# A WKV recurrence with a two-layer network behind it: pairs' exponents in PSUM, wider masks, and a written-out order of all steps

## The chip, the cores and the metric

One core of a Trainium2 chip runs the whole program. The time is device microseconds of one execution; three runs of the kernel before were taken. An execution of it was also profiled, and times inside it count from its first instruction.

## The reference

Inputs are r, k, v, w of shape (batch 4, heads 8, steps 768, 48), a bonus vector u (8, 48), and two weight matrices of 384 x 2048 and 2048 x 384. All are float32.

```python
for t in range(S):
    cur = einsum('bhd,bhe->bhde', u * k[t], v[t])
    y[t] = einsum('bhd,bhde->bhe', r[t], state + cur)
    state = w[t][..., None] * state + einsum('bhd,bhe->bhde', k[t], v[t])
x = y.transpose(0, 2, 1, 3).reshape(3072, 384)
h = x @ w_in
out = maximum(0.01 * h, h) @ w_out
```

## The kernel before

**Two stages.** The 768 steps of each batch are cut into chunks of 128, which makes 24 chunks in all. The first stage turns a chunk into 128 rows of x, transposed, in the tile `xT`. The second stage is the network: `up` (L1128) multiplies `xT` by `w_in` for a block of one or two chunks, `g` (L1143) applies the leaky function on ACT, `down` (L1155) multiplies by `w_out`, a copy (L1166 on DVE, L1168 on ACT) brings the result from PSUM to the tile `o`, and a store (L1172) sends it.

**A single chunk** (`single`, chunks 4 to 23). Four loads (L903, one each for w, k, r, v, 192 KB) fill a tile of the pool `in`, of which there are seven. ACT takes the logarithm of w (L913), PE forms cumulative sums (L919, with the totals in L922), DVE adds to make `ci` (L931), ACT takes exponentials (L945, L949; L940 for the totals), DVE multiplies r and k by them (L579, tile `rk`), and PE transposes the products (L590, with copies L595 and L597) or a transposing DMA does (L971, L1067). PE multiplies them into scores (L1076), DVE masks the scores (L995, 512 columns), PE multiplies the masked scores and the state by v (L1036, L1031). POOL computes the bonus (L611, L615, L623; the sum L619 on DVE), casts v (L631) and scales the state (L982). DVE adds the bonus (L654), and the rows are transposed into `xT` by PE (L640, copies L645, L647) or by DMA (L1052, L1089).

**A pair** (`pair`, chunks 0 and 1, then 2 and 3) does two chunks of one batch at once, the steps interleaved in two lots j = 0, 1. Its loads are L669, its logarithm L688, its cumulative sums L697 into three banks `c1`, `c0`, `cg`, its totals L714. Four exponentials (L733) follow: into a fourth bank `e0`, in place in `c1` and `cg`, and, from `c0`, into the SBUF tile `er0` of the pool `ci`. Four products (L579) read these. Then come transposes, scores (L823), masks (L834), the products with v (L781, L843), and copies (L881, L883). Pair 0 does this in two halves of two head groups (`PARTS`); both halves use the same four banks. For every half and each lot there is a scores step and two mask steps, of 256 columns in pair 0:

```python
for x, (g0, g1) in enumerate(parts):
    for js in range(2):
        ...
        for par in range(2):
            ... m.t[:, par, g0:g1, :], in0=sc[par]..., in1=mask2[:, js, :]...
```

**Weights** come in ten loads (L509 and L514 for the two matrices) through the same seven `in` tiles and are cast to bfloat16 on DVE, ACT or POOL (L533, L535, L531). An `in` tile is free again when its last reader is done.

**u** is loaded by ACT's queue, split in three (L559), spread over the partitions by three matmuls (L566), and copied (L575).

**Order.** All instructions are issued in an order fixed when the program is built. The class `Plan` runs a list scheduler over 1074 steps with written-in durations, priorities (`RANK`), some engines forced (`FORCE`), limits on banks, and a model of the DMA queue; each engine then runs its steps in that order, and SP issues loads, stores and transposing DMAs in one queue. Where the plan leaves PE idle in the first 24 us, matmuls on a tile `zeros` (L1197) are put in, into a PSUM bank held for them until the third chunk's `up`.

Of the kernel before, what the change touches and what calls it, by code (L numbers as in the profile page):

```python
# [12 lines left out]
AX = mybir.AxisListType  # L13


class Buf:


    def __init__(self, pool, kind=None, wide=1):
        self.pool, self.kind, self.users, self.t, self.free_at = pool, kind or pool, [], None, 0.0  # L20
        self.wide, self.written, self.other = wide, 0.0, 0.0


class Whole:


    def __init__(self, buf):
        self.buf = buf

    @property  # L30
    def t(self):
        return self.buf.t.rearrange("p x g t -> p (x g t)").rearrange("p (g c) -> p g c", c=256)


class Half:


    def __init__(self, buf, x):
        self.buf, self.x = buf, x

    @property
    def t(self):
        return self.buf.t[:, self.x]


class Plan:


    ENGINES = ("PE", "DVE", "ACT", "POOL", "SP")
    OVER = {"PE": 0.0, "DVE": 0.08, "ACT": 0.11, "POOL": 0.04, "SP": 0.0}  # L50
    BEGIN = {"PE": 1.1, "DVE": 2.9, "ACT": 0.8, "POOL": 4.9, "SP": 0.8}
    SEEN = {"PE": 0.21, "DVE": 0.05, "ACT": 0.05, "POOL": 0.07, "SP": 0.05}

    def __init__(self, limits, slack_from, slack, late):
        self.steps, self.limits, self.late = [], limits, late
        self.slack_from, self.slack = slack_from, slack

    def add(self, engs, fn, pri, deps=(), reads=(), takes=(), wire=None):
        i = len(self.steps)
        self.steps.append([engs, fn, pri, {d for d in deps if d is not None}, tuple(reads), tuple(takes), wire])  # L60
        for b in (*reads, *takes):
            b.users.append(i)
        return i

    def order(self, pools):
        n = len(self.steps)
        users = [[] for _ in range(n)]
        left = [len(s[3]) for s in self.steps]
        for i, s in enumerate(self.steps):
            for j in s[3]:  # L70
                users[j].append(i)
        bufs = {}
        for i, s in enumerate(self.steps):
            for b in (*s[4], *s[5]):
                bufs[id(b)] = b
        remain = {k: len(b.users) for k, b in bufs.items()}
        for b in bufs.values():
            b.written = b.other = 0.0
        free_tiles = {p: [(0.0, k) for k in range(len(t))] for p, t in pools.items()}
        in_use = {}  # L80
        ready_at = [0.0] * n
        self.start, self.done, self.eng = [None] * n, [0.0] * n, [None] * n
        free = dict(self.BEGIN)
        ready = {e: [] for e in self.ENGINES}
        events = []
        dma_free, flying = 0.0, []

        def offer(i, t):
            for e in self.steps[i][0]:
                heapq.heappush(events, (t, 0, e, i))  # L90

        for i in range(n):
            if not left[i]:
                offer(i, 0.0)
        for e in self.ENGINES:
            heapq.heappush(events, (free[e], 1, e, -1))
        count, out = 0, []
        while events:
            now, kind, e, i = heapq.heappop(events)
            same = {e}  # L100
            if kind == 0 and self.start[i] is None:
                heapq.heappush(ready[e], (self.steps[i][2], i))
            elif kind == 2:
                in_use[i] -= 1
            while events and events[0][0] <= now + 1e-9:
                _, kind, e, i = heapq.heappop(events)
                same.add(e)
                if kind == 0 and self.start[i] is None:
                    heapq.heappush(ready[e], (self.steps[i][2], i))
                elif kind == 2:  # L110
                    in_use[i] -= 1
            for e in self.ENGINES:
                if (e not in same and "*" not in same) or free[e] > now + 1e-9:
                    continue
                held, chosen = [], None
                while ready[e]:
                    pri, i = heapq.heappop(ready[e])
                    if self.start[i] is not None:
                        continue
                    ok, given, left_free = True, [], {}  # L120
                    for b in (*self.steps[i][4], *self.steps[i][5]):
                        if b.pool == "ps" and b.t is not None:
                            until = b.other if e == "PE" else b.written
                            if until > now + 1e-9:
                                heapq.heappush(events, (until, 1, e, -1))
                                ok = False
                    for b in self.steps[i][5] if ok else ():
                        if b.t is None:
                            if in_use.get(b.kind, 0) >= self.limits.get(b.kind, 99):
                                ok = False  # L130
                                break
                            if b.pool not in left_free:
                                left_free[b.pool] = {k: f for f, k in free_tiles[b.pool] if f <= now + 1e-9}
                            have = left_free[b.pool]
                            at = [(max(have[k + x] for x in range(b.wide)), k) for k in have
                                  if all(k + x in have for x in range(b.wide))]
                            if not at:
                                ok = False
                                break
                            k = min(at)[1]  # L140
                            given.append((b, k))
                            for x in range(b.wide):
                                del have[k + x]
                    if ok:
                        chosen = i
                        break
                    held.append((pri, i))
                for h in held:
                    heapq.heappush(ready[e], h)
                if chosen is None:  # L150
                    continue
                i = chosen
                engs, fn, pri, deps, reads, takes, wire = self.steps[i]
                for b, k in given:
                    gone = range(k, k + b.wide)
                    free_tiles[b.pool] = [x for x in free_tiles[b.pool] if x[1] not in gone]
                    b.slot = k
                    b.t = pools[b.pool if b.wide == 1 else b.pool + " wide"][k]
                    in_use[b.kind] = in_use.get(b.kind, 0) + 1
                d = engs[e]  # L160
                self.start[i], self.eng[i] = now, e
                out.append(i)
                count += 1
                free[e] = now + d - (self.OVER[e] if d > 0.3 else 0.0)
                if wire is None:
                    self.done[i] = now + d + self.SEEN[e]
                    if self.slack_from <= pri < 1000:
                        self.done[i] += self.slack
                else:
                    wire, size, lat, lead = wire  # L170
                    while flying and sum(x for _, x in flying) + size > 150:
                        free[e] = max(free[e], flying.pop(0)[0])
                    dma_free = max(dma_free, free[e] + lead) + wire
                    flying.append((dma_free, size))
                    self.done[i] = dma_free + lat + (self.late if now > 20 else 0.0)
                for b in (*reads, *takes):
                    if e == "PE":
                        b.written = max(b.written, self.done[i])
                    else:
                        b.other = max(b.other, self.done[i])  # L180
                heapq.heappush(events, (free[e], 1, e, -1))
                for j in users[i]:
                    left[j] -= 1
                    ready_at[j] = max(ready_at[j], self.done[i])
                    if not left[j]:
                        offer(j, ready_at[j])
                for b in {id(b): b for b in (*reads, *takes)}.values():
# [164 lines left out]
def kernel(  # L352
# [11 lines left out]
    nc = tc.nc  # L364
# [867 lines left out]
```

## Time and profile before

| | |
|---|---|
| runs | 184.61, 185.21, 202.28 us; median 185.21 |
| span of the profiled execution | 183.7 us, 5052 instructions |
| its own time | not listed apart; the two lower runs lie 0.9 and 1.5 us above its span |
| busy | PE 175.3, PEld 129.6, DVE 118.1, ACT 115.3, POOL 98.8 us |
| DMA | 34.61 MB, mean 188 GB/s; 109682 of 117131 packets under 512 B |
| HBM | read 25.17 MB, written 4.72 MB |

The span is the time between the first and the last profiled instruction; a run's time has a little around it. PE's matmuls overlap, and their ends are modelled, so a matmul's listed duration is longer than the distance to the next one. The rows name a line of the kernel, an engine, and the tiles written and read. A row with SPq is an instruction that issues a transfer; its time is how long the issue took, not the transfer.

### The profile page before, as it was taken

Reading aid. Unit: us, or ns where it says so; the run is one execution under the profiler, and the core shown is the slowest. Engines: PE = TensorE matmul, PEld = TensorE weight load, DVE = VectorE, ACT = ScalarE, POOL = GpSimd, SP = SyncE. Lnnn points to the kernel's source line nnn. Section 1 sums busy time; section 2 is a strip of 40 time slices with the busy share of each in tenths; the row PEclk is TensorE's granted clock in tenths of the full one; section 3 lists DMA queues with packets and bytes.
Section 4 is the critical chain, followed back from the end, with each engine's and each line's share of the span. In section 5 each row is a group of like instructions: output and inputs, shape, how many; then the busy total and the mean of one; then the engine's idle time right before and its main releaser. Section 6 shows DMA issues by size and latency. Waiting matters only on the chain.

```text
span 183.7 us, 5052 instructions
## 1 busy us (share of the span) xinstructions
PE 175.3 (95%) x1974; PEld 129.6 (71%) x1974; DVE 118.1 (64%) x243; ACT 115.3 (63%) x259; POOL 98.8 (54%) x134
## 2 busy tenths in 40 slices
PE   7989999999999999999999999999999999899992
PEld 2545688856778786777877877777698866686860
DVE  7498983348976989999669395867675465261000
ACT  4844989868675597687772755874589920451722
POOL 6969411225869589986676284981149547000000
PEclk9999999999999999999999999999999999999999
DMA  5999679989999999999999999999499999803202
GB/s 128 273 275 333 199 222 382 325 159 195 179 171 177 173 160 189 192 186 177 215 191 161 204 177 203 152 222 190 126 243 234 190 245 253 216 2 46 86 0 87
DMA packets 117131, 34.61 MB, mean 188 GB/s; under 512 B 109682, under 2 KB 116339, under 8 KB 117107
## 3 DMA queue, kind: packets, MB, share of 16 engines
q1 hardware_dynamic: 117104, 34.28, 90.6%
q8 instruction: 15, 0.25, 0.6%
q14 instruction: 10, 0.07, 0.1%
q10 hardware_dynamic: 2, 0.00, 0.0%
HBM read 25.17 MB, written 4.72 MB: 163 GB/s over the span
## 4 chain that ended last, share of the span: by engine, by line
PE 56%; DMA 15%; SPq 9%; ACT 6%; DVE 6%; issue 4%; POOL 2%; DVEq 0%; POOLq 0%; ACTq 0%
PE ps L1128 23%; PE ps L1155 19%; SPq L903 9%; DMA in<-in_w_dram 5%; DMA in<-in_r_dram 4%; DMA in<-in_v_dram 4%; PE ps L1197 3%; DVE rk L579 2%; DMA xT<-y 2%; ACT g L1143 2%; PE ps L1076 2%; PE ps L1036 1%; PE ps L1031 1%; PE ps L919 1%; PE ps L823 1%
## 5 line engine op out<-in xcount | busy, mean ns | idle before, releaser
L1155 PE MATMUL ps<-w_out_b,g 128*128 128x384 bf16 x384 | 70.8, 326 | 0.1
L1128 PE MATMUL ps<-xT,w_in_b 128*128 128x256 bf16 (+1 forms) x672 | 69.4, 258 | 0.7 <-DMA xT<-y 0.7
L1143 ACT ACTIVATE g<-ps 128x512 bf16<-128x512 f32 x96 | 54.5, 605 | 20.3 <-PE ps L1128 16.4
L1128 PEld LDWEIGHTS <-w_in_b 128*128 128x128 bf16 x672 | 57.1, 98 | 9.0 <-DMA xT<-y 1.1
L1155 PEld LDWEIGHTS <-g 128*128 128x128 bf16 x384 | 34.8, 97 | 19.9 <-ACT g L1143 0.5
L579 DVE TENSOR_TENSOR rk<-in,ps 128x384 bf16<-128x384 f32 (+1 forms) x49 | 25.1, 525 | 11.3 <-DMA in<-in_r_dram 4.1
L995 DVE TENSOR_TENSOR m<-ps,maskb 128x512 bf16<-128x512 f32 x40 | 25.1, 683 | 9.1 <-PE ps L1076 9.1
L611 POOL TENSOR_TENSOR ru<-in,ub 128x384 f32<-128x384 f32 x24 | 23.9, 999 | 6.7 <-DMA in<-in_k_dram 6.5
L615 POOL TENSOR_TENSOR ru<-ru,in 128x384 f32<-128x384 f32 x24 | 24.3, 1016 | 3.1 <-DMA in<-in_r_dram 2.6
L623 POOL TENSOR_TENSOR vs<-in,dg 128x384 f32<-128x384 f32 x20 | 16.5, 828 | 10.9 <-DMA in<-in_v_dram 4.8
L982 POOL TENSOR_TENSOR sb<-s,a 128x384 bf16<-128x384 f32 x18 | 14.9, 829 | 13.3 <-ACT a L940 13.1
L1168 ACT COPY o<-ps 128x384 f32<-128x384 f32 x13 | 6.2, 478 | 15.5 <-PE ps L1155 15.4
L631 POOL CAST vb<-in 128x384 bf16<-128x384 f32 x24 | 12.1, 509 | 7.1 <-DMA in<-in_v_dram 7.1
L931 DVE TENSOR_TENSOR ci<-ps,lw 128x384 f32<-128x384 f32 x20 | 11.0, 554 | 7.0 <-PE ps L922 5.4
L619 DVE TENSOR_REDUCE dg<-ru 128x8 f32<-128x384 f32 x24 | 13.0, 547 | 3.6 <-POOL ru L615 3.5
L654 DVE TENSOR_TENSOR y<-ps,vs 128x384 bf16<-128x384 f32 x20 | 10.8, 553 | 3.1 <-PE ps L1036 1.7
L913 ACT ACTIVATE lw<-in 128x384 bf16<-128x384 f32 x20 | 10.2, 521 | 3.8 <-DMA in<-in_w_dram 3.7
L940 ACT ACTIVATE a<-ps 64x4 f32<-64x4 f32 x36 | 6.1, 168 | 9.1 <-DVE ci L931 6.0
L590 PE MATMUL ps<-ident,rk 128*128 128x128 bf16 x88 | 9.4, 235 | 1.8 <-DVE rk L579 1.7
L949 ACT ACTIVATE ps<-ci 128x384 f32<-128x384 f32 x20 | 9.8, 488 | 0.5 <-DVE ci L931 0.5
L945 ACT ACTIVATE ps<-ps 128x384 f32<-128x384 f32 x20 | 9.4, 472 | 0.5
L1166 DVE COPY o<-ps 128x384 f32<-128x384 f32 x11 | 6.1, 554 | 5.1 <-PE ps L1155 5.0
(89 smaller groups left out, 177.5 us busy)
## 6 DMA issues: line engine op xcount, KB each, us to landing
out_dram<-o SPq DMA_DIRECT2D x24, 192.0 KB, 3.5
in<-in_w_dram SPq DMA_DIRECT2D x22, 192.0 KB, 4.5
in<-in_k_dram SPq DMA_DIRECT2D x22, 192.0 KB, 4.4
in<-in_r_dram SPq DMA_DIRECT2D x22, 192.0 KB, 4.2
in<-in_v_dram SPq DMA_DIRECT2D x20, 192.0 KB, 4.1
in<-in_moe_w_out_dram SPq DMA_DIRECT2D x4, 768.0 KB, 9.3
in<-in_moe_w_in_dram SPq DMA_DIRECT2D x2, 768.0 KB, 6.8
in<-in_moe_w_in_dram SPq DMA_DIRECT2D x4, 384.0 KB, 7.8
```

The source lines that it names most:

```text
L579: (nc.gpsimd if e == "POOL" else nc.vector).tensor_tensor(out=o, in0=x, in1=i, op=ALU.mult)
L611: lambda e: nc.gpsimd.tensor_tensor(out=ru.t[:], in0=kv(), in1=ubv, op=ALU.mult),
L615: lambda e: nc.gpsimd.tensor_tensor(out=ru.t[:], in0=ru.t[:], in1=rv(), op=ALU.mult),
L619: lambda e: nc.vector.tensor_reduce(out=dg.t[:], in_=ru.t[:], axis=AX.X, op=ALU.add),
L623: lambda e: nc.gpsimd.tensor_tensor(out=vs.t[:], in0=vv(), in1=dg.t[:].unsqueeze(2).to_broadcast([128, H, D]), op=ALU.mult),
L631: {"POOL": 0.56}, lambda e: nc.gpsimd.tensor_copy(out=vb.t[:], in_=vv()),
L903: nc.sync.dma_start(out=part(i)(), in_=src[b, :, t0 : t0 + L, :].rearrange("h p d -> p h d"))
L982: lambda e: nc.gpsimd.tensor_tensor(out=sb.t[:].rearrange("p g a d -> p (g a) d"), in0=s_in.t[:].rearrange("p g a d -> p (g a) d"), in1=a_ ...
L995: lambda e, par=par: nc.vector.tensor_tensor(out=m.t[:, par, :, :], in0=sc[par].t[:].rearrange("p (g t) -> p g t", g=NP), in1=maskb[:].uns ...
L1128: nc.tensor.matmul(hp.t[:, a * N : (a + 1) * N].rearrange("p (s n) -> p s n", n=L), lhsT=w_in_b[:, t, (j + a) * 128 : (j + a + 1) * 128], ...
L1143: lambda e, hp=hp, g=g, j=j, J=J, N=N: nc.scalar.activation(out=g.t[:, j : j + J, 0:N], in_=hp.t[:, 0 : J * N].rearrange("p (a n) -> p a n ...
L1155: nc.tensor.matmul(op.t[:, 0:DM], lhsT=g.t[:, j, off : off + 128], rhs=w_out_b[:, j, :], start=(j == 0), stop=(j == NJ - 1))
```

## The change

The file is written anew around the same steps; this is what differs in what the chip is told to do.

**Pairs' exponents all in PSUM.** The exponential of `c0` is taken in place.

```diff
-er0 = Buf("ci")
-s_r0 = exp(c0, er0, 1.0, [s_c0[x]], [c0], [er0], *P)
+s_r0 = exp(x, c0, c0, 1.0, [s_c0], [])
```

**A bank per half.** Each half of pair 0 has four banks of its own, and its own transposed pieces begin at column 0 of their bank.

```diff
-c1, c0, cg, e0 = (Buf("ps", "cp2") for _ in range(4))
-for x, (g0, g1) in enumerate(parts):
+for x in range(len(parts)):
+    c1, c0, cg, e0 = (Bf("ps", "cp2") for _ in range(4))
```

**Masks of 512 columns.** In pair 0, one scores step of a half now does both lots, into two banks, and two masks of 512 columns follow where there were four of 256. Pair 2 keeps its four masks of 512. The two `m` tiles of a pair are neighbours.

```diff
-ms, scs, s_ms = [Buf("m"), Buf("m")], [[Buf("ps", "sc"), Buf("ps", "sc")] for js in range(2)], {}
+mb = Bf("m", wide=2)
...
+cuts = [(0, 2)] if half else [(0, 1), (1, 2)]
...
+mult(e, mb.t[:, :, par, g0:g1, :],
+     sc[par].t[:].rearrange("p (j g t) -> p j g t", j=2, t=128),
+     mask2[:].unsqueeze(2).to_broadcast([128, 2, g1 - g0, 128]))
```

**u's product.** The matmuls and the copy for u have no priority of their own any more; the table places them. The fillers' bank is released by a step that the table places too, not by the third chunk's `up`.

**The order as a table.** `Plan`, `RANK`, `FORCE` and the limits are gone. Two constants replace them: `TABLE` names 1068 steps in order, each with the engine that runs it (P, V, A, G, S for PE, DVE, ACT, POOL, SP) and, as Z words, eleven filler matmuls; `HOMES` names for every buffer the tile of its pool. Its first lines:

```python
TABLE = """
A0 S11 P1066 S6 A1 S9 S7 S8 V2 S10 V3 S12 Z512 Z512 Z512 Z512 Z512 Z512 Z256 Z192 P4 S88 A13 Z128 P16 V5 P17 A27
P15 A26 S153 A14 A24 Z512 Z160 P18 V31 G58 A25 P19 V28 A40 P21 S89 A43 V37 G62 P32 A41 V44 P29 A22 V53 P1067 P38
...
P86 V148 A87 P110 G118 S149 A111 P740 S159 A146 G122 P129 V119 P132 V131 A741 P732 S162 G116 V134 P730 G120 A733
```

`P740` is the first `up`, `P129` and `P132` are pair 2's scores; `S153`, `S147`, `S145`, `S151`, `S156` and `S149` are the loads of `w_in`, `S159`, `S162`, `S165` and `S168` those of `w_out`. In this order the cast of the first `up`'s weights and one other of `w_in` are on POOL (`G155`, `G154`); three of `w_out` are there too, where two were. Stores stand in SP's queue soon after their copies: eight are ahead of the w load of chunk 15, where one was, and 17 ahead of the last load, where 14 were.

A further switch, `FAST`, for another way to compute `down`, is an empty set, so that code is not used.

More of the change, by code (lines that the diff above doesn't have):

```diff
@@ L63, in add @@
         return i
[L65 to L187, printed above, removed]
-                    b.free_at = max(b.free_at, self.done[i])
-                    remain[id(b)] -= sum(u == i for u in b.users)
-                    if remain[id(b)] == 0:
-                        free_tiles[b.pool] += [(b.free_at, b.slot + x) for x in range(b.wide)]
-                        heapq.heappush(events, (b.free_at, 2, "*", b.kind))
-        if count != n:
-            raise RuntimeError(("stuck", count, n, [(self.steps[i][0], self.steps[i][2]) for i in range(n) if self.start[i] is None][:20]))
-        return out
@@ L1185 @@
[L1185 to L1201 removed]
+                        "down", "PE", down, (nb, 32 + i * 8 + q),
@@ new lines, in product, with go, gj, sj @@
+        def product(bank, a, b_, first, at, deps, reads):
+            def go(e):
+                for j in range(HJ):
+                    mm(bank.t[:, 0:HN], a(j), b_(j), first and j == 0, j == HJ - 1)
+            return step("half", "PE", go, (nb, at), deps=deps, reads=reads, takes=[bank])
+        def gj(i, j2, g=g):
+            return lambda j: g.t[:, HJ * j2 + j, L * i : L * (i + 1)]
+        def sj(i, sq=sq):
+            return lambda j: sq(i)[:, j, :]
+        def wj(i, j2):
+            return lambda j: w_out_b[:, HJ * i + j, HN * j2 : HN * (j2 + 1)]
@@ L1205, with zero @@
+    for n in range(NCH):
+        if n >= LEAD and n in lns:
+            st.steps[lns[n]][7].append(up_first[n - LEAD])
+    warm = Bf("ps", "warm")
+    step("warm", "PE", lambda e: None, takes=[warm])
+    step("cold", "PE", lambda e: None, 99, reads=[warm], soft=[ends[0]])
+    def zero(n):
+        mm(warm.t[:, 0:n], zeros[:, 0:128], zeros[:, 0:n], True, True)
+    with tc.manual_schedule():
+        constants()
+        st.issue(TABLE, [int(x, 36) for x in HOMES], pools, zero)
 _INS = ['r', 'k', 'v', 'w', 'u', 'moe_w_in', 'moe_w_out']
```

1372 lines of the change are left out of this document (677 added, 695 removed), and 133 rows, old and new, of the table RANK.

## The prediction

> **What bounds the kernel now.** I read the page's busy times first, then windows, then the timeline of the opening, and last the chain of waits.
>
> ```profile
> span 183.7 us, 5052 instructions
> PE 175.3 (95%) x1974; PEld 129.6 (71%) x1974; DVE 118.1 (64%) x243; ACT 115.3 (63%) x259; POOL 98.8 (54%) x134
> ```
>
> ```profile
> 20.00:22.00 2.00, 1.77 (x47) 1.29 (x44) 1.72 (x4) 2.00 (x5) 0.41 (x1) 1.00 0.48 158
> 22.00:24.00 2.00, 2.00 (x30) 1.32 (x28) 2.00 (x5) 2.00 (x5) 1.24 (x2) 1.00 0.06 16
> 24.00:26.00 2.00, 2.00 (x49) 1.46 (x47) 2.00 (x4) 1.41 (x3) 0.00 (x0) 1.00 0.90 195
> ...
> 12.00:16.00 4.00, 4.00 (x42) 1.88 (x35) 3.39 (x10) 0.66 (x2) 3.52 (x5) 1.00 1.12 321
> ...
> 60.00:80.00 20.00, 19.30 (x250) 14.90 (x248) 18.56 (x40) 13.74 (x37) 17.28 (x23) 1.00 1.12 181
> 80.00:100.00 20.00, 20.00 (x242) 15.29 (x239) 16.14 (x33) 12.54 (x31) 13.95 (x19) 1.00 1.11 185
> 100.00:120.00 20.00, 20.00 (x241) 16.03 (x240) 14.19 (x29) 14.28 (x35) 12.57 (x16) 1.00 1.03 185
> ```
>
> The columns are the stretch, its length, the busy time of PE, PEld, DVE, ACT and POOL, the granted clock, the DMA share and GB/s. Two resources are full at once. PE is busy nearly throughout, and the DMA share is 1.03 to 1.12 from 60 to 120. Only at 20 to 26 do the DMA engines run dry: (1 - 0.48) x 2 + (1 - 0.06) x 2 + (1 - 0.90) x 2 = 3.1 us of transfer time is lost.
>
> ```profile
> 8.46 1.21 DVE L579 TENSOR_TENSOR rk<-in,ci 128x192 bf16<-128x192 f32 x1
> 9.59 0.60 DVE L579 TENSOR_TENSOR rk<-in,ps 128x192 bf16<-128x192 f32 x2
> ...
> 16.46 1.40 DVE L579 TENSOR_TENSOR rk<-in,ci 128x384 bf16<-128x384 f32 x1 [0.91 <-ACT ci L733]
> ...
> 20.61 0.92 ACT L647 COPY xT<-ps 128x384 bf16<-128x384 bf16 x2
> 21.35 1.62 ACT L535 CAST w_in_b<-in 128x768 bf16<-128x768 f32 x2
> 22.30 0.83 PE L1128 MATMUL ps<-xT,w_in_b 128*128 128x256 bf16 x6
> ...
> 15.80 0.82 SPq L509 DMA_DIRECT2D in<-in_moe_w_in_dram  x1
> 23.00 0.37 SPq L514 DMA_DIRECT2D in<-in_moe_w_out_dram  x1
> ```
>
> The first product of the second stage (`up`, L1128) starts at 22.30, after xT of pair 0 is copied (to 21.53) and a cast of the first weights on ACT. SP issues no weight load between 15.80 and 23.00: all seven `in` tiles are taken, and the next comes free with the second of those ACT casts, at 21.35 + 1.62 = 22.97. That is the DMA hole above.
>
> ```profile
> 65.45 4.74 DMA in<-in_r_dram
> ...
> 76.45 0.40 PE ps L590 x4
> ...
> 153.22 4.37 DMA xT<-y
> 157.64 2.79 PE ps L1128 x24
> ...
> 175.55 4.57 PE ps L1155 x28
> 180.14 0.48 ACT o L1168
> ```
>
> In the chain that ended last, loads of inputs set the pace up to about 76; from there to 180.14 PE's own work does, but for one transfer ending at 157.6. So an earlier start is worth something only as far as the loads come earlier too.
>
> **The change part by part.** The real matmuls are the same ones. Counted in the built program's order, PE has 14 fewer, all of them fillers on `zeros` (25 to 11). Behind the first `up` both orders hold the same steps, except that the changed one has pair 2's two `scores` there as well. So PE's work after its start hardly changes, and two questions are left: when the first `up` starts, and how much PE waits after it.
>
> *Exponents in PSUM.*
>
> ```profile
> L579 DVE TENSOR_TENSOR rk<-in,ci 128x192 bf16<-128x192 f32 x2 | 1.8, 915 | 0.0
> L579 DVE TENSOR_TENSOR rk<-in,ps 128x192 bf16<-128x192 f32 x6 | 1.9, 347 | 2.6 <-ACT ps L733 2.6
> L579 DVE TENSOR_TENSOR rk<-in,ci 128x384 bf16<-128x384 f32 x1 | 1.4, 1402 | 0.9 <-ACT ci L733 0.9
> L579 DVE TENSOR_TENSOR rk<-in,ps 128x384 bf16<-128x384 f32 x43 | 23.1, 550 | 8.8 <-DMA in<-in_r_dram 4.1 <-ACT ps L949 1.8 <-DMA out_dram<-o 0.8
> L834 DVE TENSOR_TENSOR m<-ps,mask 128x256 bf16<-128x256 f32 x8 | 2.8, 415 | 0.2 <-PE ps L823 0.2
> L834 DVE TENSOR_TENSOR m<-ps,mask 128x512 bf16<-128x512 f32 x4 | 2.7, 684 | 0.1
> ```
>
> Three products that read the exponent from SBUF become products that read it from PSUM: 2 x (915 - 347) = 1.14 us and 1402 - 550 = 0.85 us less on DVE, which is busy 3.39 of the 4 us from 12 to 16. That PSUM products keep their speed beside POOL is seen at 9.59, where two took 0.60 while POOL's L615 ran. The exponentials themselves change only their output tile.
>
> *Masks.* Eight of 256 columns become four of 512: 8 x 415 - 4 x 684 = 0.58 us less on DVE, just before pair 2's products. A mask now waits for both score groups of its half, at most 0.4 us later; the others queued on DVE cover that.
>
> *A bank per half.* Each half of pair 0 takes four banks, so all eight are in use, and the filler's bank is given up once pair 0's totals are done. The second half's cumulative sums and the transposes queue for banks; the price is at worst a wait for an exponential or a copy, and since PE waits on DVE there anyway I take nothing, with 0.5 us as the bound.
>
> *Order of the opening.* Pair 2's cumulative sums stand ahead of pair 0's last scores, no longer behind 2 us of filler, so DVE's 0.91 us wait at 16.46 goes. DVE's path is shorter by 1.14 + 0.85 + 0.58 + 0.91 = 3.48 us. Two casts of `w_in`, among them that of the first `up`, move to POOL.
>
> ```profile
> L531 POOL CAST w_out_b<-in 128x768 bf16<-128x768 f32 x2 | 2.0, 1020 | 10.8 <-DMA in<-in_moe_w_out_dram 10.8
> ...
> 14.08 0.50 POOL L631 CAST vb<-in 128x384 bf16<-128x384 f32 x1
> 14.55 1.95 POOL L611 TENSOR_TENSOR ru<-in,ub 128x384 f32<-128x384 f32 x2
> ```
>
> POOL's eight steps for pair 0 end at 14.58; then a cast, two products, and the cast: 14.58 + 1.02 + 1.95 + 1.02 = 18.6. The first `up` needs this and xT (21.53 - 3.48 = 18.05). I take 19.0, that is 3.3 us earlier; bounds 1.7 us (only the 1.14 and 0.58 arrive) and 3.7 us (POOL's 18.6).
>
> *The order of the loads.* With the weight casts spread over POOL, DVE and ACT, the `in` tile that SP waits for comes free with POOL's second cast, at about 18.6 and not 22.97, while transfers are still under way, so most of the 3.1 us hole closes. I take 2.6. Against this stand the stores: four outputs are now sent before the last k or r load of chunks 10 and 11, where none was, and two loads fewer.
>
> ```profile
> out_dram<-o SPq DMA_DIRECT2D x24, 192.0 KB, 3.5
> in<-in_r_dram SPq DMA_DIRECT2D x22, 192.0 KB, 4.2
> ...
> 70.37 0.80 SPq L903 DMA_DIRECT2D in<-in_r_dram  x1
> ...
> 77.84 0.62 PE L1076 MATMUL ps<-rkT 48*128 48x128 bf16 x16
> ```
>
> A load of 192 KB at 181 GB/s is 1.06 us; a store costs between 192 KB at the 321 GB/s of 12 to 16, 0.6 us (nearest, for its rows are long too), and the same 1.06. So 4 x 0.6 - 2 x 1.06 = +0.3 us: 2.3 us is left of the gain. The tightest place is scores of chunks 10 and 11: chunk 11's r was issued at 70.37 and landed 4.2 us later, 74.6; the scores ran at 77.84, 3.2 us behind it. The way between (product 0.55, transposes 0.4, copy 0.4, signals and DVE's queue) needs some 2, so 1.2 is to spare. But the new order reaches these scores with 1.6 us less PE work since the first `up` (27 `down` steps before them, not 30, the rest making up 0.3). PE can thus come 2.3 + 1.2 - 1.6 = 1.9 us earlier here; the other 1.4 of the 3.3 turns into waiting. From 80 on PE is full, and the gain is carried to the end.
>
> *Everything else* (u's product, tiles fixed by a table, copies that change engine) moves work between engines that are busy 54 to 64%, at no cost to PE.
>
> **Sum.** 183.7 - 1.9 = 181.8 us of span. The runs shown are 184.61 and 185.21 without the long one, so 0.9 to 1.5 us lie around the span of the profiled execution; on the median, 183.3 us.
>
> **The rivals.**
>
> *Loads keep up* (0.14). If stores cost nothing beside the loads and 0.69 us of wait for xT before 157.64 goes as well, the whole 3.3 arrives: 185.2 - 3.3 - 0.7 = 181.2. For: PE's waits from 60 to 80 (0.70) are its last but for that one. Against: the 1.6 us that the new order asks for earlier.
>
> *A slow PE at the start* (0.22).
>
> ```profile
> 13.27 2.00 PE L1197 MATMUL ps<-zeros 128*128 128x512 bf16 x5
> 15.06 0.85 PE L697 MATMUL ps<-lw,tinc 128*128 128x384 bf16 x2
> 16.27 0.49 PE L697 MATMUL ps<-lw,tstr 128*128 128x384 bf16 x2
> ```
>
> The window's clock column reads 1.00 from 0 on, but two matmuls of 384 columns take 0.85 us at 15.06 and 0.49 at 16.27. PE goes at about half pace until some 3 us of unbroken matmuls, from 13.27, are done; the 2 us of filler in them are gone in the new order. If PE enters the second stage at half pace for 3 us, 1.5 us are lost, twice that if it happens again: 183.3 + 1.5 = 184.8. Against: pair 2's sums and pair 0's products now follow each other closely from about 11 to 15.
> The Trainium skill ("TensorE: Matmul & The Clock Gate", Part 1) says that full rate comes after one free-running window of about 3.4 us in which PE was busy, and goes after an idle one. The row agrees in size. By it a start in the half-rate state would cost an estimated 1.7 us, or 3.4 where the window is missed once.
>
> *The queue of transfers starves PE* (0.15, slower).
>
> ```profile
> 88.67 3.15 SPq L1067 DMA_TRANSPOSE rkT<-rk  x1
> ```
>
> SP issues in order, and the new order has eight stores ahead of chunk 15's w load where there was one, and this transpose of some 3 us as well, which was behind it. Each store waits for its copy, and with it all loads behind. If a store costs as much as a load (1.06) and POOL's second cast is late, so that the hole stays, that w comes 7 x 1.06 = 7.4 us later by the stores alone. The order asks for its sums 3.0 us of PE work later, so 4.4 us become PE's wait: 185.2 + 4.4 = 189.6. It decides from the point where the hole isn't closed; with it closed the same sum is 187. For: the DMA share of 1.11 from 80 to 100 leaves no room. Against: stores were nearer to 0.6 in the sum above, which takes 3.2 us off.
>
> *The change does nothing* (0.05): the start stays near 22, since ACT's exponentials, not DVE, set it; 185.2. Against: ACT is busy 0.66 of 4 us at 12 to 16.
>
> **How the numbers follow.** The forecast, 183.3, has 0.44, its own range 181.8 to 184.6 (start gain 1.7 to 3.7, hole 2 to 3.1). The range of all, 180.9 to 187.6, leaves out the far part of the starving queue and little of the first rival. 2% is 3.7 us, about what a measurement of this kernel can tell from no change. Faster than 181.5: the first rival and a little of the forecast, 0.15. Slower than 188.9: most of the starving queue, 0.12. The rest is 0.73.
>
> **What would show it.** Right: no `rk<-in,ci` for pairs; the first L1128-like matmul at 18.6 to 20; no DMA share under 0.7 between 8 and 40; PE waits of 1 to 2 us in sum for `rk` or `lw` between 45 and 75; the last matmul at about 178. Wrong: 256-column matmuls at twice their pace after 19 (the second rival); DMA share still low at 20 to 24; PE waits over 3 us in sum between 60 and 110 with stores before them in SP's queue (the third); or a first `up` after 21.

## The result, and the profile after

| | before | after |
|---|---|---|
| median of 20 runs each | 184.65 us | 181.92 us |
| profiled execution: its time, its span | about 185.5, 183.7 us | 181.88, 180.1 us |
| first `up` starts | 22.30 us | 18.84 us |

The ratio of the times is 0.990, with a 95% interval of 0.9872 to 0.9928: 1.0% faster, and within the 2% that counts as the same. By the medians it is 2.7 us, 1.5%. The forecast was 183.3 us. The time of a run lies about 1.8 us above its span (181.88 against 180.1), so the profiled execution of before was a long one, 0.9 us above its median. The ratio leaves out runs more than 1.5% above the fastest of the same kernel, which are nine of before's twenty here and most of them in the last two groups of experiments, so I read medians of all runs beside it (184.34 and 184.35 us for before in those two groups).

Of the kernel after, the page's first lines, then windows with the columns of the prediction:

```profile
span 180.1 us, 5012 instructions
PE 171.3 (95%) x1960; PEld 128.1 (71%) x1960; DVE 112.2 (62%) x230; ACT 118.6 (66%) x265; POOL 101.3 (56%) x137
```

```profile
20.00:22.00 2.00, 2.00 (x34) 1.73 (x24) 1.88 (x4) 1.72 (x4) 1.09 (x2) 1.00 1.05 364
22.00:24.00 2.00, 1.60 (x56) 1.16 (x55) 1.62 (x3) 1.50 (x3) 1.44 (x3) 1.00 1.08 371
24.00:26.00 2.00, 2.00 (x25) 1.78 (x23) 1.91 (x4) 1.90 (x4) 0.00 (x0) 1.00 1.04 373
...
40.00:60.00 20.00, 19.63 (x285) 15.38 (x284) 16.37 (x32) 14.47 (x34) 14.90 (x21) 1.00 1.08 198
60.00:80.00 20.00, 19.94 (x255) 15.70 (x253) 16.66 (x33) 16.71 (x41) 15.57 (x18) 1.00 1.02 200
80.00:100.00 20.00, 20.00 (x230) 15.41 (x229) 13.76 (x28) 13.98 (x35) 13.85 (x18) 1.00 1.14 186
100.00:120.00 20.00, 19.41 (x232) 14.76 (x230) 15.10 (x28) 11.69 (x29) 12.27 (x16) 1.00 0.99 201
```

The DMA share at 20 to 26, which was 0.48, 0.06 and 0.90, is now 1.04 to 1.08: the hole is closed. PE is no longer short from 60 to 80 (19.94, it was 19.30), but it is at 22 to 24, at 40 to 60 and at 100 to 120.

The groups of DVE's first 24 us, kernel after (count, busy time and mean ns, then the idle time ahead):

```profile
L231 DVE TENSOR_TENSOR m<-ps,mask 128x512 bf16<-128x512 f32 x8 | 5.2, 685 | 1.1 <-PE ps L242 1.1
L231 DVE TENSOR_TENSOR rk<-ps,in 128x192 bf16<-128x192 f32 x8 | 2.5, 350 | 1.4 <-ACT ps L456 1.3
L231 DVE TENSOR_TENSOR rk<-ps,in 128x384 bf16<-128x384 f32 x4 | 2.1, 550 | 0.0
```

All products of the pairs take the PSUM price, 350 and 550 ns. The timeline of the kernel after, where a bracket tells how long the engine idled ahead and for whom:

```profile
6.41 0.77 PE L242 MATMUL ps<-zeros 128*128 128x512 bf16 x2
...
11.82 0.48 PE L242 MATMUL ps<-lw,tinc 128*128 128x384 bf16 x2 [0.67 <-ACT lw L417]
...
16.81 0.84 POOL L235 CAST w_in_b<-in 128x768 bf16<-128x768 f32 x1
...
18.31 0.48 ACT L239 COPY xT<-ps 128x384 bf16<-128x384 bf16 x1
...
18.84 0.81 PE L242 MATMUL ps<-xT,w_in_b 128*128 128x256 bf16 x6 [0.24 <-ACT xT L239]
...
19.30 2.25 SPq L299 DMA_DIRECT2D in<-in_moe_w_out_dram  x3
...
22.70 0.52 PE L242 MATMUL ps<-vb,rk 64*128 64x96 bf16 x16 [0.40 <-POOL vb L235]
50.17 0.40 PE L353 MATMUL ps<-ident,rk 128*128 128x128 bf16 x4 [0.34 <-DVE rk L231]
117.67 2.58 PE L242 MATMUL ps<-xT,w_in_b 128*128 128x256 bf16 x22 [0.59 <-DMA xT<-y]
```

The first `up` follows the copy of xT on ACT (18.31 + 0.48 = 18.79), and POOL's cast was over at 17.65. SP issues the loads of `w_out` from 19.30 on, where it stood until 23.00. One row was not expected: two matmuls of 384 columns take 0.48 us at 11.82 already, the full pace. Before, they took 0.85 at 15.06. And of the 3.46 us that the first `up` comes earlier, some 0.6 are pair 2's scores, which stood ahead of it before (21.07 to 21.71) and stand behind it now (19.58 to 20.22).

### The profile page after: what moved, and what is told of

Its sections match the earlier page's. It is cut to its first block, busy times and chain, and to the rows that moved or that the text cites. A ratio compares the mean times of both kernels' runs of the same rounds, so it can differ in the third digit from the quotient of the medians.

```text
span 180.1 us, 5012 instructions
## 1 busy us (share of the span) xinstructions
PE 171.3 (95%) x1960; PEld 128.1 (71%) x1960; DVE 112.2 (62%) x230; ACT 118.6 (66%) x265; POOL 101.3 (56%) x137
## 4 chain that ended last, share of the span: by engine, by line
PE 61%; DMA 12%; ACT 7%; POOL 6%; DVE 5%; issue 5%; SPq 2%; POOLq 0%; DVEq 0%; ACTq 0%
PE ps L242 59%; DMA in<-in_w_dram 6%; DMA in<-in_r_dram 3%; POOL ru L231 3%; DMA xT<-y 2%; DVE rk L231 2%; DVE m L231 2%; ACT g L858 2%; PE ps L353 1%; SPq L618 1%; ACT ps L651 1%; POOL sb L231 1%; POOL vs L231 1%; ACT lw L626 1%; POOL vb L235 1%
## 5 line engine op out<-in xcount | busy, mean ns | idle before, releaser
L242 PE MATMUL ps<-xT,w_in_b 128*128 128x256 bf16 (+1 forms) x672 | 70.6, 257 | 0.9 <-DMA xT<-y 0.6
L858 ACT ACTIVATE g<-ps 128x512 bf16<-128x512 f32 x96 | 56.4, 597 | 14.5 <-PE ps L242 12.3
L231 DVE TENSOR_TENSOR rk<-ps,in 128x384 bf16<-128x384 f32 (+1 forms) x52 | 26.2, 520 | 7.9 <-ACT ps L651 2.6
L231 POOL TENSOR_TENSOR ru<-ru,in 128x384 f32<-128x384 f32 x24 | 23.8, 1001 | 0.8
L239 ACT COPY o<-ps 128x384 f32<-128x384 f32 x19 | 9.1, 480 | 16.1 <-PE ps L242 16.0
L242 PEld LDWEIGHTS <-rkT 48*128 48x128 bf16 (+2 forms) x304 | 10.6, 97 | 3.5 <-issue 1.7
```

The lines of the kernel that those rows point to most:

```text
L231: (nc.gpsimd if e == "POOL" else nc.vector).tensor_tensor(out=o, in0=a, in1=b, op=op)
L239: nc.scalar.copy(out=o, in_=i)
L242: nc.tensor.matmul(o, lhsT=a, rhs=b, start=start, stop=stop, skip_group_check=True)
L858: lambda e, hp=hp, g=g, j=j, J=J, N=N: nc.scalar.activation(out=g.t[:, j : j + J, 0:N], in_=hp.t[:, 0 : J * N].rearrange("p (a n) -> p a n ...
```

## The experiments

Two theories stood against each other. *Loads*: the gain hangs on the closed hole, and the early start pays only as far as the loads follow. *Start*: the first `up` alone sets the time. For every kernel the start is taken from the profiled execution, and so is PE's idle time from there to 176 us. In e7 and e10 the start is the first useful `up`. The medians are of all runs, and runs of one kernel differ in PE's pace at the start (the experiments e1 to e10 show this), so a row's start and its median need not belong together; its start, idle time and span do.

| kernel | first useful `up` | PE idle behind it | hole | span | median of runs |
|---|---|---|---|---|---|
| before | 22.30 | 1.72 | open | 183.7 | 184.34 to 184.66 |
| e3_hole | 20.80 | 2.91 | open | 184.5 | 185.33 |
| after, and its control | 18.84, 18.81 | 1.55, 1.91 | closed | 180.1, 180.5 | 181.92, 182.66 |
| e2_mask256 | 18.90 | 1.53 | closed | 180.3 | 182.33 |
| e8_both | 19.39 | 1.13 | closed | 180.3 | 182.79 |
| e6_more_filler | 19.87 | 0.62 | closed | 179.6 | 182.88 |
| e8b_xt_first | 20.36 | 1.01 | closed | 180.7 | 182.87 |
| e5_no_late_filler | 20.51 | 0.17 | closed | 179.6 | 182.20 |
| e9_combined | 20.91 | 1.00 | closed | 181.1 | 182.70 |
| e4_late_stores | 20.93 | 0.96 | closed | 180.9 | 182.13 |
| e10_half_late | 22.4 | 0.53 | closed | 182.1 | 183.92 |
| e1_sbuf | 22.50 | 0.24 | closed | 181.8 | 184.02 |
| e7_late_start | 22.6 | 0.59 | closed | 182.2 | 184.93 |

Three of the windows behind the idle times, for before, after and e5 (length less busy time of PE):

```profile
22.30:176.00 153.70, 151.98 (x1730) 116.47 (x1730) 100.98 (x194) 100.65 (x224) 81.98 (x102) 1.00 0.94 187
18.84:176.00 157.16, 155.61 (x1783) 119.30 (x1783) 97.65 (x185) 106.16 (x234) 85.81 (x106) 1.00 0.93 187
20.51:176.00 155.49, 155.32 (x1785) 119.25 (x1784) 96.98 (x185) 105.71 (x234) 84.53 (x105) 1.00 0.91 186
```

**c0_after**, the changed kernel again, for the comparison on one chip.

> The changed kernel itself, to have its time beside the others on one chip. Theory and rival alike: 181.9 us, 0.988 to 0.993 of the time before; the first `up` at 18.6 to 19.2 us.

Measured: 182.66 us (12 runs; before 184.66 beside it), ratio 0.9909, interval 0.9876 to 0.9941, first `up` at 18.81. The waits of PE are not those of the first profile. There is none at 50 any more, and one more at 110:

```profile
20.78 0.50 POOL L235 CAST vb<-in 128x384 bf16<-128x384 f32 x1 [1.40 <-DMA in<-in_v_dram]
...
22.57 0.52 PE L242 MATMUL ps<-vb,rk 64*128 64x96 bf16 x16 [0.30 <-POOL vb L235]
...
109.52 0.52 ACT L626 ACTIVATE lw<-in 128x384 bf16<-128x384 f32 x1 [1.93 <-DMA in<-in_w_dram]
110.10 0.32 PE L242 MATMUL ps<-lw,trev 128*128 128x384 bf16 x1 [0.45 <-ACT lw L626]
...
118.11 2.14 PE L242 MATMUL ps<-xT,w_in_b 128*128 128x256 bf16 x18 [0.87 <-DMA xT<-y]
```

The first two go back to loads: POOL idled 1.40 us for v ahead of the first of its two casts, and ACT 1.93 us for w ahead of the logarithm. So loads take back a part of an early start, and where they do it varies from run to run.

**e1_sbuf**: the exponential of `c0` goes to SBUF again.

```diff
-s_r0 = exp(x, c0, c0, 1.0, [s_c0], [])
+er0 = pools["ci"][n // 2]
+s_r0 = step("exp2" + half, "ACT", ... activation(out=er0[:, 2 * g0 : 2 * g1, :], ...
...
-mult(e, rk[j].t[...], heads(bank.t)[:, h0:h1, :], ...)
+mult(e, rk[j].t[...], (er0[:] if bank is c0 else heads(bank.t))[:, h0:h1, :], ...)
```

> One part undone: the exponential of c0 is written to an SBUF tile again, for pair 0's halves and pair 2, in the changed order. Theory (DVE's chain of products sets the first `up`): the three SBUF products take 2 x 915 and 1402 ns instead of 347 and 550, so the first `up` comes 1.2 to 2.0 us later than 18.84, at 20.0 to 20.8, and the time rises by 1 to 2 us, to 182.9 to 183.9. Rival (the start is set by something else, POOL's casts or PE's rate): the products are as long, but the first `up` moves less than 0.4 us and the time less than 0.4.

Groups and timeline of e1:

```profile
L231 DVE TENSOR_TENSOR rk<-ci,in 128x192 bf16<-128x192 f32 x2 | 1.5, 742 | 0.1
L231 DVE TENSOR_TENSOR rk<-ci,in 128x384 bf16<-128x384 f32 x1 | 1.4, 1431 | 0.0
```

```profile
5.41 0.45 PE L242 MATMUL ps<-zeros 128*128 128x512 bf16 x2
7.64 0.32 PE L242 MATMUL ps<-lw,tstr 128*128 128x192 bf16 x1 [1.79 <-ACT lw L417]
...
13.20 0.80 PE L242 MATMUL ps<-lw,tinc 128*128 128x384 bf16 x2 [0.33 <-ACT lw L417]
...
22.50 0.82 PE L242 MATMUL ps<-xT,w_in_b 128*128 128x256 bf16 x6 [0.27 <-ACT xT L239]
```

Measured: 184.02 us, 1.36 above the control by medians. The ratio, 0.9948 with 0.9903 to 0.9992, is 0.4% above the control's, and the intervals overlap, so the sign is likely and the size is not settled. The start came at 22.50, later than the 20.0 to 20.8 expected, for this profile ran at half pace. It shows more, if PE's pace is kept apart. Here PE had its full pace early (two fillers in 0.45 us at 5.41, 0.77 in the kernel after), idled 1.79 us, and then ran the 384-column matmuls at half pace (0.80 at 13.20). e4 had the same opening at the same pace (0.80) and started at 20.93. So the SBUF products cost about 22.50 - 20.93 = 1.57 us of start. Their rows give 2 x (742 - 350) + (1431 - 547) = 1.67, with e4's 547 for the PSUM product. (By the clock of the windows PE was back at full pace some 2.6 us later in e1 than in e4, so a part of the 1.57 may be pace.)

**e2_mask256**: pair 0's masks in eight pieces.

```diff
-mult(e, mb.t[:, :, par, g0:g1, :], sc[par]..., mask2[:].unsqueeze(2)...)
+for j in range(2):
+    mult(e, mb.t[:, j, par, g0:g1, :], sc[par]...[:, j], mask2[:, j, :].unsqueeze(1)...)
```

> One part undone: pair 0's masks are eight of 256 columns again, in the changed order. Theory (each 0.1 us of DVE's chain ahead of the first `up` counts): 8 x 415 - 4 x 684 = 0.58 us more on DVE, the first `up` 0.3 to 0.6 us later than in the changed kernel at the same PE pace (18.84 at full pace, 20.9 where PE is at half pace from 8 to 18), the time 0.3 to 0.5 us up on the changed kernel's 182.7 of the runs beside it. Rival (there is slack on DVE before the products): first `up` and time within 0.2 us.

Groups of DVE's first 24 us and timeline of e2:

```profile
L231 DVE TENSOR_TENSOR m<-ps,mask 128x256 bf16<-128x256 f32 x8 | 2.9, 417 | 0.6 <-PE ps L242 0.6
L231 DVE TENSOR_TENSOR m<-ps,mask 128x512 bf16<-128x512 f32 x4 | 2.6, 684 | 0.3 <-PE ps L242 0.3
```

```profile
18.90 0.82 PE L242 MATMUL ps<-xT,w_in_b 128*128 128x256 bf16 x6 [0.24 <-ACT xT L239]
```

Measured: 182.33 us, and the first `up` 0.06 us later at the same pace (0.48 us for the two matmuls at 11.83). The rival is right. The 0.58 us were never there in full: a mask starts before the listed end of the one ahead, so the sum of durations counts time twice. By busy time the narrow masks cost 2.9 + 2.6 - 5.2 = 0.3 us more. Of that, 0.2 lies in time that DVE spends waiting anyway: with wide masks it waits 1.1 us for scores, with narrow ones 0.9.

**e3_hole**: the first three loads of `w_out` wait for the `in` tile that pair 2 holds.

```diff
 HOMES: the two `in` tiles of S159 and S171 exchanged, and so for their later users
 TABLE:
-... P740 S159 A146 ... P732 S162 ... V126 S165 P138 P135 S171 ...
+... P740 A146 ... P732 ... V126 P138 P135 S159 S162 S165 S171 ...
```

> The hole in the transfers made anew, the opening's work left as it is: the first three loads of w_out wait for the tile that pair 2's v or r holds, so that SP can issue nothing from some 16 to 22 us. Theory (the early start is worth something only because the loads come earlier too): the DMA share falls to under 0.6 in a stretch of 2 to 4 us between 18 and 26, the first `up` stays at 18.8 +- 0.3, and the lost 1.5 to 2.5 us of transfer time come back as PE's waits between 25 and 75, total +1.3 to +2.5 us (183.2 to 184.4). Rival (the loads have slack, the start alone counts): the total rises by less than 0.5 us.

Windows, timeline of SP's queue and of PE, e3:

```profile
22.00:24.00 2.00, 2.00 (x34) 1.70 (x22) 1.92 (x4) 1.53 (x4) 0.64 (x3) 1.00 0.52 171
24.00:26.00 2.00, 1.89 (x62) 1.49 (x60) 2.00 (x4) 2.00 (x4) 0.83 (x1) 1.00 0.06 12
26.00:28.00 2.00, 2.00 (x22) 1.81 (x20) 1.86 (x4) 1.77 (x5) 0.00 (x0) 1.00 0.82 240
```

```profile
14.32 3.68 SPq L301 DMA_DIRECT2D in<-in_moe_w_in_dram  x3
24.86 2.15 SPq L301 DMA_DIRECT2D in<-in_moe_w_out_dram  x3
```

```profile
20.80 0.81 PE L244 MATMUL ps<-xT,w_in_b 128*128 128x256 bf16 x6 [0.43 <-ACT xT L241]
...
31.15 1.46 PE L244 MATMUL ps<-w_out_b,g 128*128 128x384 bf16 x8 [0.20 <-POOL w_out_b L237]
```

The hole has the size that it had before: 0.96 + 1.88 + 0.36 = 3.2 us of transfer time lost, against 3.1. Measured: 185.33 us, 2.7 above the control; ratio 1.0047, interval 1.0008 to 1.0086, wholly above the control's. That is a little above the theory's 1.3 to 2.5 and far from the rival's 0.5. The profiled execution went at half pace in the opening, so its start is 20.80 and not 18.8. With a start 1.5 us earlier than before's, this kernel is no faster than before. (It opens the hole some 2 us later than before and holds up the first `down` as well, so 2.7 is an upper size for the hole alone.)

**e4_late_stores**: the eight stores ahead of chunk 15's w load go behind S729, the last but five of SP's transfers.

```diff
 TABLE: S757 S785 S779 S799 S751 S813 S835 S841 moved right behind S729
```

> Eight stores that stand ahead of chunk 15's w load in SP's order are put behind it and its companions. Theory (stores ahead of loads are what is left of the waits from 45 to 75): a store costs the loads behind it some 0.6 us, PE's waits at 49.7, 57.7 and 68.6 (0.50, 0.19 and 0.22 us) go, and the time falls by 0.5 to 0.9 us, to 181.0 to 181.4. Rival (stores cost the loads nothing, or the waits come back in other places): within 0.3 us of 181.9.

Timeline of e4, PE and then SP's queue:

```profile
12.25 0.80 PE L243 MATMUL ps<-lw,tinc 128*128 128x384 bf16 x2 [0.30 <-ACT lw L418]
...
20.93 0.81 PE L243 MATMUL ps<-xT,w_in_b 128*128 128x256 bf16 x6 [0.50 <-ACT xT L240]
```

```profile
163.73 14.56 SPq L831 DMA_DIRECT2D out_dram<-o  x13
```

Measured: 182.13 us (6 runs), ratio 0.9888, interval 0.9841 to 0.9934. That is 0.5 us under the control, with wide overlap. The edit goes further than a place just behind that load: the eight stores are issued together with the last five, from 163.73 on, where the control has only those five. Without them the DMA share from 80 to 100 is 0.92, 1.09 in the control, and the time hardly follows. PE is full from 40 to 60, but in the control it nearly was too (19.94), with the stores where they were. The theory isn't shown; whether a store costs the loads anything stays open.

**e5_no_late_filler** and **e6_more_filler**: PE's pace in the opening.

```diff
 TABLE, e5:
-... A13 Z128 P16 ... A24 Z512 Z160 P18 ...
+... A13 P16 ... A24 P18 ...
 TABLE, e6:
-... A24 Z512 Z160 P18 ...
+... A24 Z512 Z160 Z512 Z512 Z512 Z512 P18 ...
```

> The three fillers behind the first eight (columns 128, 512 and 160) are left out; nothing else. Theory (PE's pace in the opening hangs on these: without them PE idles at 6.4 us in every run and goes at half pace from about 8 to 18): the granted clock is 0.96 to 0.975 in nearly all runs, none at 1.0; the first `up` at 20.5 to 21.2; the time 182.4 to 182.8, some 0.5 us above the runs of the changed kernel that have a clock of 1.0. Rival (the half pace comes and goes by itself): clocks spread from 0.97 to 1.0 as in the changed kernel, time as there.

> Four more fillers of 512 columns follow the two at 6.4 us. Theory (a gap of 1.4 us in PE's work at 6 to 7.5 is what drops the pace to a half until 18 us): no run has a stretch at half pace behind 9 us, clocks 0.99 to 1.0, the first `up` at 18 to 19.5; runs in which full rate comes late pay up to 4 x 0.43 = 1.7 us for the fillers themselves, so the median time lies at 181.5 to 182.5 and no run of the low-clock kind is left. Rival (the half pace comes and goes by itself): clocks from 0.97 to 1.0 as before, time 0 to 1 us longer.

Window and timeline of e5:

```profile
8.00:12.00 4.00, 3.33 (x35) 2.23 (x36) 3.72 (x12) 3.07 (x9) 4.00 (x6) 0.51 1.15 311
```

```profile
20.51 0.81 PE L242 MATMUL ps<-xT,w_in_b 128*128 128x256 bf16 x6 [0.35 <-ACT xT L239]
```

Measured: e5 182.20 us (6 runs), e6 182.88 (7 runs), both outside their theory's range. On the clocks the theory fell in both. Of e5's six runs three show a mean granted clock of 0.999 or 1.0, and three of e6's seven show 0.981. (A mean clock near 1.0 is no proof of full pace, as e10 shows below.) The profiled run of e5 did go at half pace from 8 (0.51), so a gap in PE's work may bring it, but it isn't the whole of it. More telling is the time. e5's profiled run began the second stage 1.67 us later than the kernel after, and its span is 0.5 us shorter: PE idles 0.17 us behind the start, where it is 1.55 in the kernel after. In these two profiles PE waits later for most of what it starts before 20.5 us. e8b, e9 and e4, with starts from 20.4 to 20.9 and some 1.0 us of idle time, show less of it.

**e7_late_start** and **e10_half_late**: PE alone is kept busy longer ahead of the second stage.

```diff
-for a in range(J):
+for a in [0] * (10 if (c0, j) == (0, 10) else 0) + list(range(J)):    # e10: 5
     for t in range(KT):
         mm(hp.t[:, a * N : (a + 1) * N]..., w_in_b[...], xT[...], a == 0 and t == 0, t == KT - 1)
```

> The first `up` forms its first sum eleven times instead of once: 30 more matmuls of 256 columns, 30 x 107 = 3.2 us of PE work at the start of the second stage; loads and all other engines as they are. Theory (the loads set the pace up to about 75 us, so an earlier start alone turns partly into waiting): the waits at 49.7, 57.7 and 68.6 us (0.9 us in sum) go, and the hole stays closed, so the time rises by 2.0 to 2.4 us, not 3.2. Rival (the start alone is what counts): +3.0 to 3.3 us. Third case (the loads hold far more than the visible waits): below +1.5.

> The late start at half its size: 15 more matmuls of 256 columns in the first `up`, 1.6 us. The runs so far give, for the first useful `up` at 18.8, 20.9 and 22.5 us, some 182.0, 182.5 and 184.0 us. Theory (a knee near 21 us: what PE starts earlier than that it waits later): with full pace, a start at 20.4, within 0.4 us of the changed kernel, 181.9 to 182.4; with half pace, a start at 22.5, 183.6 to 184.1. Rival (each us of start is a us of time): +1.6 in both, 183.5 and 184.2.

Timeline of e7, then a window and the timeline of e10:

```profile
19.29 4.09 PE L242 MATMUL ps<-xT,w_in_b 128*128 128x256 bf16 x36 [0.24 <-ACT xT L239]
```

```profile
12.00:16.00 4.00, 4.00 (x59) 2.17 (x59) 2.35 (x6) 2.14 (x6) 3.09 (x6) 1.00 1.17 284
```

```profile
11.93 0.80 PE L242 MATMUL ps<-lw,tinc 128*128 128x384 bf16 x2 [0.30 <-ACT lw L417]
...
20.02 0.61 PE L353 MATMUL ps<-ident,rk 128*128 128x128 bf16 x4
...
20.74 2.48 PE L242 MATMUL ps<-xT,w_in_b 128*128 128x256 bf16 x21
```

In e7 the added matmuls end at 19.29 + 4.09 - 0.81 = 22.6. Its span is 182.2, 1.7 above the control's and 2.1 above the first profile of the kernel after; its median is 2.3 us above the control and 2.6 above e2, which ran beside it. That is nearer to the theory's 2.0 to 2.4 than to the rival's 3.0 to 3.3. By the median the kernel is no faster than before (184.93 against 184.34), with the hole closed. That median mixes paces: the six runs with a mean clock of 0.996 or more have a median of 183.96, the six at 0.972 or less 185.26. (Its start is 0.3 us later than before's, and pair 2's scores, 0.6 us, stand behind the start now; so at before's own start the closed hole may bring up to 1 us.) In e10 the start was at 20.74 and the useful one at 22.4, and its run took 183.87 us, within the 183.6 to 184.1 expected for a start at 22.5. The rival had 184.2 there, too close to tell apart, and no run at full pace was profiled; so the knee rests on the table, not on e10. There it is a bend rather than a knee: PE's idle time falls from 1.5 to 1.9 us at starts near 18.8 to between 0.2 and 1.0 at 20.4 to 20.9, and to between 0.2 and 0.6 at 22.4 to 22.6.

**e8b_xt_first**, **e8_both**, **e9_combined**: the wait at 117 us.

```diff
 TABLE, all three:
-... P515 S562 P903 V516 ... A919 S523 P574 ... V591 P563 V924 P938 V564 S925 P934 V572 ...
+... P515 P903 V516 S523 S562 ... A919 P574 ... V591 V924 P938 S925 P934 P563 V564 V572 ...
 e8 and e9: and the stores of e4;  e9: and without the fillers of e5
```

> Only the order of two transposing transfers in SP's queue: the xT transfer of chunks 14 and 15 goes ahead of the r/k transposition of chunks 16 and 17, whose scores go behind two more `up` steps. Theory (the last large wait of PE, 0.8 to 1.1 us at 116.9 for xT, is the queue's order and not the loads): xT lands some 3 us earlier, that wait goes, no new one above 0.3 comes, the time falls by 0.6 to 0.9 us, to 181.5 to 182.0. Rival (loads set the pace there too): the wait turns up at the scores or behind, time within 0.3 us of the changed kernel's 182.3 to 182.7.

> The same together with the eight late stores. Theory (each wait is its own, and an early first `up` pays once the waits behind it go): 181.0 to 181.6 us. Rival: 182.0 to 182.6, as with the late stores alone.

> The same as the last, and without the three fillers behind the first eight. Theory (an `up` at 20.5 us is early enough, and the fillers bring nothing): 180.8 to 181.6 us, some 3 us below the kernel before. Rival (an `up` at 20.5 is late once the waits are gone): 0.5 to 1.5 us above the last kernel, 182 to 182.8.

Timeline of e8b:

```profile
117.07 1.47 PE L243 MATMUL ps<-xT,w_in_b 128*128 128x256 bf16 x12 [0.29 <-DVE rk L232]
119.65 1.47 PE L243 MATMUL ps<-xT,w_in_b 128*128 128x256 bf16 x12 [0.56 <-DVE m L232]
```

Measured: 182.87, 182.79 and 182.70 us. The wait for xT is gone, and 0.29 and 0.56 stand in its place, for a product (`rk`) and a mask (`m`) on DVE. For e8b the rival is right: moving one transfer only moves the wait. e8_both came out 0.2 above its rival's range, and e9, level with e8_both, lies inside its rival's 182 to 182.8 but not 0.5 to 1.5 above e8_both, as that rival had it. No kernel tried beats the changed one by more than the error (the lowest medians, 182.13 and 182.20, have 6 runs each and stand beside 182.66 and 182.33), so there is no better version to offer.

## Why the prediction was right, and where it was not

**The frame was right.** It said that an earlier start is worth something only as far as the loads come earlier too. Four kernels show it: late start and hole, 184.65 (before); earlier start and hole, 185.33 (e3); late start without the hole, 184.93 (e7); early start without it, 181.92. (e10 and e1, without the hole and with starts at 22.4 and 22.5, lie 0.4 and 0.6 us under the before beside them.) Neither part alone brings more than a fraction of the gain; both together bring 2.7 us by medians, 1.8 by the ratio, where 1.9 was forecast.

**The hole** was to be worth 2.6 us; undone in the changed order it costs 2.7. Since 2.7 is an upper size, some of the agreement is luck. It closed for the reason given, an `in` tile that comes free earlier, but by another cast: POOL's second was over at 17.65, and by the profile SP's issue at 19.30 waited for one on DVE that ended at 19.27.

**The start** was forecast at 19.0 and came at 18.84, but by terms that do not hold one by one, so the agreement is luck. The products were priced at 1.14 + 0.85 = 1.99; at like pace they are worth about 1.57. The masks' 0.58 is 0.06; the rows of before that it was taken from already had busy times of 2.8 and 2.7 us, only 0.1 apart. The 0.91 for the wait shows nowhere: e1, which has the new order and the wide masks but not the PSUM products, starts at 22.50 at half pace, and before started at 22.30. So the step "DVE's path is shorter by 3.48" was some 1.6 in fact, in an opening at half pace. What made up the rest was PE's pace, which had no term in the sum. e10 has the changed kernel's opening at half pace, as before had (0.80 us for the two matmuls at 11.93), and starts at 20.74, 1.56 earlier than before. (Before was at full pace by 16.27, e10 not yet at 20.02, so at equal pace it may be somewhat more.) The kernel after had full pace by 11.82 and came 1.9 earlier still. Nor did the sum take off the 0.6 us of scores that moved behind the start. The POOL bound of 18.6 did not bind: the cast took 0.84, not 1.02, and was over at 17.65.

**What is given back.** I said that 1.4 us of the gain would turn into waiting, at scores of chunks 10 and 11, between 45 and 75. In sum none did in these two profiles: PE's idle time behind the start is 1.55 us, and it was 1.72. Waits that before had are gone (0.70 from 60 to 80, 0.69 from 140 to 160), and others came: 0.40 at 22.70, 0.34 near 50 and 0.59 at 117.67; the control's late ones are at 110 and 118. The sign named for it, 1 to 2 us of waits for `rk` or `lw` between 45 and 75, came to 0.34. An early start does bring new waits, as 1.55 beside e5's 0.17 shows, but the old ones that went make up for them, and the gain by medians is 2.7, not 1.9. The sum behind the 1.4 had 4 x 0.6 for the stores, which is not supported: e4 took eight stores away from there and moved the time by 0.5 us, inside the error.

**The base.** The profiled span of before was taken as 0.9 to 1.5 us below a run's time; it is 1.8, and that execution was 0.9 us longer than the median. From 184.65 the same 1.9 would have given 182.75.

**The rivals.** A slow PE at the start is real, but not as I priced it. It acts before the first `up`, not in the second stage; it moves the start by some 2 us (18.8 or 20.9 in the same opening) and the time by less than 1: the kernel after's nine runs with a mean clock of 0.981 or less have a median of 182.35 us, the other eleven 181.77. The starving queue did not come: at 80 to 100 the DMA share is 1.14 and PE is busy all 20.00 us. Loads that keep up had a gain of 4.0 us; the 2.7 by medians lies between that and the forecast's 1.9, nearer the forecast. The wait before 157.64 did go, as this rival had it, but waits at 22.70, 50 and 117.67 came. The change that does nothing would have left the start at 22.

## What to carry to other kernels

Where two resources are full at once, price an earlier start and an earlier load together, and test them apart by delaying each alone: here the hole alone took the whole gain away, and the late start alone all or most of it. Read what a shorter chain on one engine brings from the step that waits for it, not from the sum of shorter instructions: of 0.58 us of masks, half was overlap counted twice, and most of the rest went into a wait that was there anyway. And compare starts only between profiles in which the same matmul takes the same time.

## What the runs showed of the hardware

One opening runs at several paces from execution to execution. In the kernel after, e2 and e7, the two 384-column matmuls took 0.48 us near 11.9; in e1, e4 and e10 they took 0.80. In e1 the fillers before them had been at full pace and the half pace came after an idle stretch of 1.79 us; in e10 PE had been busy without a break (4.00 of the 4 us from 4 to 8) and was at half pace all the same. The openings of the kernel after and of e10 are alike to 0.1 us up to 8.2, and yet the one has its full pace by 9.3 and the other not yet at 20.02. What decides it is not settled: leaving fillers out (e5) or adding some (e6) did not fix it. The Trainium skill ("TensorE: Matmul & The Clock Gate", Part 1) says that the window in which PE's activity is judged runs freely, so that the moment of full pace shifts with where the first matmul falls in it, by about half a microsecond. The runs agree that it shifts from run to run. They show a larger shift: PE was at full pace at 5.41 in e1 and at 11.82 in the kernel after, and still at half pace at 11.93 in e10. Nor does e10 bear out the rule that the prediction drew on, that full rate follows one busy window of about 3.4 us: PE was busy for all of 4 to 8 and of 12 to 16 there.

The granted clock of the windows does not always show this. In every profile the first 4 us read 1.00, though the eight fillers of 512 columns in them took 2.96 to 3.12 us and two such fillers later in e1 0.45. For e10 it reads 1.00 at 12 to 16 with the matmuls at 0.80, as it did for before; for e5 it reads 0.51 at 8 to 12. The duration of a known matmul is the safer sign.

The SBUF product of 192 columns took 742 ns in e1 and 915 before, with the same operands; that of 384 columns 1431 and 1402. One product on POOL in before, then one on POOL and one on DVE in e1:

```profile
16.46 0.99 POOL L615 TENSOR_TENSOR ru<-ru,in 128x384 f32<-128x384 f32 x1
```

```profile
8.92 1.12 POOL L231 TENSOR_TENSOR ru<-in,ub 128x384 f32<-128x384 f32 x1
9.38 0.88 DVE L231 TENSOR_TENSOR rk<-ci,in 128x192 bf16<-128x192 f32 x1
```

All six SBUF products of the two kernels overlap a product on POOL, and each ends at the same distance behind it, however early it began: 0.21 to 0.22 us with 192 columns (10.26 behind 10.04 here), 0.42 with 384 (17.86 behind 17.45 for the one of 1.40 us at 16.46). So most of their length is a wait for POOL, and the 1.14 and 0.85 us that the prediction took from it depend on what POOL does just then. The Trainium skill ("GPSIMD Engine Reference", 8. Key points) says that POOL shares its way into SBUF with DVE's instructions of two SBUF inputs; the rows agree. No run has an SBUF product beside an idle POOL. The PSUM products stayed at 350 and 550 with POOL at work beside them.
